# A fifth place for probabilities, half key blocks and interleaved query features in a four-layer attention kernel

## The chip, the cores and the metric

The kernel runs on one core of a Trainium2 chip. The metric is the device time of one execution in microseconds (us); several runs are taken and their median is used. The engines are named as in the profile: PE (TensorE) multiplies, PEld is its weight load, DVE (VectorE), ACT (ScalarE) and POOL (GpSimd) work element by element, SP (SyncE) issues most transfers.

## The reference

Four residual blocks follow one another on 2048 tokens of 512 features: A, B, A, B, with the same weights for both A and for both B. There are 32 heads of 16 features.

```python
def _A_ref(x, wqkv, wo):          # linear attention
    q, k, v = heads(x @ wqkv)
    phi = lambda t: jnp.where(t > 0, t + 1, jnp.exp(t)) + 1e-6
    pq, pk = phi(q), phi(k)
    kv = jnp.einsum("bhsd,bhse->bhde", pk, v)
    z = jnp.einsum("bhsd->bhd", pk)
    num = jnp.einsum("bhqd,bhde->bhqe", pq, kv)
    den = jnp.einsum("bhqd,bhd->bhq", pq, z)[..., None] + 1e-6
    return merge(num / den) @ wo

def _B_ref(x, wqkv, wo):          # causal attention in a window of 256
    q, k, v = heads(x @ wqkv)
    scores = jnp.einsum("bhqd,bhkd->bhqk", q, k) * (Dh ** -0.5)
    mask = (i - j >= 0) & (i - j < 256)
    p = _softmax(jnp.where(mask, scores, -1e9), axis=-1)
    return merge(jnp.einsum("bhqk,bhkd->bhqd", p, v)) @ wo

x = x + _A_ref(_layernorm(x), A_wqkv, A_wo)
x = x + _B_ref(_layernorm(x), B_wqkv, B_wo)
x = x + _A_ref(_layernorm(x), A_wqkv, A_wo)
x = x + _B_ref(_layernorm(x), B_wqkv, B_wo)
```

## The kernel before

The tokens are 16 tiles of 128. A Python class (`Plan`) lists every operation of the program with its engine or engines, what it reads and writes, and its PSUM banks (`Tile`); nothing loops on the chip. The order of all operations, the engine of each that has a choice, and the bank of each PSUM tile are not computed: they are read from a table of bytes packed in the source (`TABLE`, unpacked in `place`), so a new table is a new schedule. `synchronise` then puts the semaphore waits in. `WIDE` names DVE operations behind which POOL operations of a later place in the order wait.

The stages, with the lines of the profile:

- **First layer (A), keys** (`layer_a_keys`, 0 to about 47 us): for each tile a layer norm, transposed; key features (`tok`, L406) through phi (ACT L429, DVE L430 and L431), and sums over tokens (L481, L504). Query features (`feat`, L420) have the 128 features of one chunk on the partitions, chunk f being heads 8f to 8f+7.
- **Barrier** (`barrier`): the masked kv sum times the output weights gives a matrix M (one product for each chunk, L527; copied by L395). For each group G of four tiles the denominators are made in four column tiles of PE (L543), inverted (L547, L548) to 32 heads x 128 tokens per tile, and spread over the partitions by PE: 16 products on 32-row tiles fill four PSUM banks, one for each tile of tokens (L556). DVE multiplies the query features by that (L563, PSUM source).
- **Second layer (B), together with the next A keys** (`middle(2)`): for tile j the result of A is added (`a_out`, L406 and L574), normed and transposed by a DMA, and projected (L420). `b_scores` makes scores of 64 keys x 256 queries for two feature groups and two 64-key blocks on 32-row tiles (L638), exponentials over 1024 columns (ACT L648) into a place `P(j % rp)`, and the diagonal's mask (POOL L657 or DVE L658). `b_far` makes the last 64 queries of each key block's window (L712, exponentials L725, mask L743 or L744). `b_values` multiplies probabilities and values: for each of 16 head pairs one product for each of up to six key blocks of 64 keys x 2 heads (L764, 128 queries as weights, 34 columns: two heads of 16 values and a one). In the first block after the diagonal and in the farthest, half of the 128 queries meet zeros kept in columns 320 to 384 of each row. Then a reciprocal and a division (L775, L776), a transpose by DMA, the output product and the residual (L406, L574).
- **Second barrier**, then the **last layer (B)** (`middle(3)`): as above, but with `merged` set: the near scores skip 32 queries (224 instead of 256, exponentials of 896 columns), and `b_far` computes these with the far ones on 32-row, 64-column tiles (L715), twice as many products; DVE puts the near part in its place under the mask (L735). The probabilities have `rp = 4` places here, three in their own buffer and one (`P(3)`, tile name vp) over the finished keys and values of layer A.

SP's DMAs are one queue in program order: kB and vB copies of keys and values (L600, L619), transposes (L377), outputs (L931).

Of the kernel before, what the change touches and what calls it, by code (L numbers as in the profile page):

```python
# [11 lines left out]
P = 128  # L12
# [76 lines left out]
WIDE = ("E1", "xn", "mk", "mf")  # L89
# [128 lines left out]

def bass_view(x, free):

    return bass.AP(x.tensor, x.offset, [x.ap[0]] + free)


class Plan:
# [83 lines left out]
    def consts(self, after):  # L308
# [11 lines left out]
        pool("c4", lambda e: e.affine_select(out=K.bmask[:], in_=K.bmask[:], compare_op=ALU.is_ge, fill=0.0, base=0, pattern=[[-16, 8], [0, 16]], channel_multiplier=1), 152, 300, rd=[("bmask",)], wr=[("bmask",)])  # L320
        pool("c5", lambda e: e.affine_select(out=K.bmask[:], in_=K.bmask[:], compare_op=ALU.is_ge, fill=0.0, base=15, pattern=[[16, 8], [0, 16]], channel_multiplier=-1), 153, 300, rd=[("bmask",)], wr=[("bmask",)])

        pool("c6", zero(lambda: K.hot, 1.0), 154, 200, wr=[("hot",)])
        pool("c7", lambda e: e.affine_select(out=K.hot[:], in_=K.hot[:], compare_op=ALU.is_ge, fill=0.0, base=0, pattern=[[128, 4], [-16, 32]], channel_multiplier=1), 155, 300, rd=[("hot",)], wr=[("hot",)])
        pool("c8", lambda e: e.affine_select(out=K.hot[:], in_=K.hot[:], compare_op=ALU.is_ge, fill=0.0, base=15, pattern=[[-128, 4], [16, 32]], channel_multiplier=-1), 156, 300, rd=[("hot",)], wr=[("hot",)])
        pool("c9", zero(lambda: K.spread), 157, 1750, wr=[("spread",)])
        for tg in range(4):
            pool("c10", lambda e, tg=tg: e.affine_select(out=K.spread[:], in_=K.spread[:], compare_op=ALU.not_equal, fill=1.0, base=-32 * tg, pattern=[[-8, 4], [-1, 8], [0, 16]], channel_multiplier=1), 158, 760, rd=[("spread",)], wr=[("spread",)])
# [116 lines left out]
    def a_q(self, t, key):  # L445
        K = self
        ps = self.feat("q", t, lambda c, f: K.wA[:, c, f * P:(f + 1) * P], lambda c: K.XQ[:, c, t * P:(t + 1) * P], [("XQ", t), ("wAq",)], key)
        self.phi(ps, lambda: K.XQ[:, :, t * P:(t + 1) * P], [("XQ", t)], key + 0.1, 1)

    def a_kv(self, t, kv, z, key):  # L450
        K = self

        def put(e):
# [4 lines left out]
            for f in range(4):  # L458
                fs = slice(f * P, (f + 1) * P)
                m = e.matmul(K.ps(z)[:, f:f + 1], K.pk[:, t, fs], K.ones[:, 0:1], start=t == 0 and f == 0, stop=t == T - 1, skip_group_check=True)  # L460
# [4 lines left out]
    def layer_a_keys(self, ph, base):  # L465
# [33 lines left out]
        for q in range(4):  # L499
            def put(e, q=q):  # L500
                m = None
                for t in range(4 * q, 4 * q + 4):
                    for f in range(4):
                        m = e.matmul(K.ps(z)[:, f:f + 1], K.pk[:, t, f * P:(f + 1) * P], K.ones[:, 0:1], start=t == 0 and f == 0, stop=t == T - 1, skip_group_check=True)  # L504
# [5 lines left out]
    def barrier(self, ph):  # L510
# [12 lines left out]
        self.on("DVE", "kvm", lambda e: e.tensor_tensor(K.pqd[:, :, :], K.ps(kv).rearrange("p (f n) -> p f n", f=4), K.bmask[:].unsqueeze(1).to_broadcast([P, 4, P]), ALU.mult), key - 2, dve(512), rd=[("bmask",)], wr=[("pqd",)], ps=[kv])  # L523
        self.on("DVE", "zs", lambda e: e.tensor_tensor(K.zs[:], K.hot[:], K.ps(z)[:, 0:4].unsqueeze(2).to_broadcast([P, 4, 32]), ALU.mult), key - 2, dve(128), rd=[("hot",)], wr=[("zs",)], ps=[z])
        for f in range(4):
            ps = Tile(1, K.cls)
            self.pe("M", lambda e, f=f, ps=ps: e.matmul(K.ps(ps), K.pqd[:, f, :], K.wAo[:, f, :], start=True, stop=True), key - 2 + f * 0.01, 1, 512, rd=[("pqd",), ("wAo",)], ps=[ps])  # L527
            self.copy("Me", ps, lambda f=f: K.M[:, f, :], lambda ps=ps: K.ps(ps), key - 2 + f * 0.01, 512, wr=[("M", f)])
        for G in range(4):
# [19 lines left out]
            bc = [Tile(1, "S") for _ in range(4)]  # L549

            def put(e, G=G, bc=bc):
                m = None
                for f in range(4):
                    for tg in range(4):
                        rows = slice(32 * tg, 32 * tg + 32)
                        m = e.matmul(K.ps(bc[tg])[:, f * P:(f + 1) * P], K.spread[rows, f, :], K.rec[rows, G, :], start=True, stop=True, tile_position=(32 * tg, 0))  # L556
                return m

            self.pe("spread", put, k + 0.2, 1, 512, occ=245, mode=(32, 128), rd=[("rec", G), ("spread",)], ps=bc)
            for tg in range(4):  # L560
                t = 4 * G + tg
                x = lambda t=t: K.XQ[:, :, t * P:(t + 1) * P]
                self.on("DVE", "pqd", lambda e, x=x, b=bc[tg]: e.tensor_tensor(x(), K.ps(b).rearrange("p (f n) -> p f n", f=4), x(), ALU.mult), k + 0.3 + 0.01 * tg, dve(512), rd=[("XQ", t)], wr=[("XQ", t)], ps=[bc[tg]])  # L563
# [131 lines left out]
    def b_far(self, j, key):  # L695
# [33 lines left out]
        for fs in ((0, 1), (2, 3)) if merged else ():  # L729
            for b in range(2):  # L730
                def mk(e, b=b, fs=fs):
                    x = bass_view(K.P(sl)[:, fs[0], 0, 384 * b + 288:384 * b + 320], [[704, 8], [-256, 2], [1, 32]])
                    o = bass_view(K.P(sl)[:, fs[0], 0, 384 * b:384 * b + 64], [[704, 8], [32, 2], [1, 32]])
                    t = K.tri[:, 0, :].rearrange("p (a n) -> p a n", a=2).unsqueeze(1).to_broadcast([P, 8, 2, 32])
                    return e.tensor_tensor(o, x, t, ALU.mult)  # L735

                self.on("DVE", "mk", mk, key + 0.02 + 0.01 * b + 0.2 * fs[0], dve(512, "2x"), rd=[("P", sl, f, b, h) for f in fs for h in range(2)] + [("F", sl, 0), ("F", sl, 1), ("tri",)],
                        wr=[("P", sl, f, b, 2) for f in fs] + [("near", sl, b, fs[0])])
        for b in range(2):
# [7 lines left out]
            self.g.add("mf", engs, mk, key + 1.5 + 0.01 * b, rd=[("F", sl, 0), ("F", sl, 1), ("tri",)] + [("near", sl, b, 0), ("near", sl, b, 2)] * merged, wr=[("F", sl, b, 1)])  # L747

    def b_values(self, j, h, key):
# [23 lines left out]
        s = j % 2  # L773
# [380 lines left out]
```

## Time and profile before

| | |
|---|---|
| median of 3 runs | 406.92 us (406.59 to 408.15) |
| profiled execution, first to last instruction | 405.4 us |
| PE busy | 386.1 us, 95%, 7930 instructions |
| DVE busy | 333.6 us, 82%, 759 |
| ACT busy | 341.5 us, 84%, 439 |
| POOL busy | 149.2 us, 37%, 243 |
| granted PE clock | full throughout |

The profiled execution is one run of the program; its span leaves out about 1.5 us that the timed runs hold around it. Matmuls are pipelined and their ends modelled, so the start of the next instruction tells more of PE than the length of one. A mean share of busy time hides stages of different kind, so the profile is read by stretches. Numbers like L764 are lines of the kernel; in a group of instructions the columns are count, busy us, mean ns of one, and the idle time before them with what ended it.

### The profile page before, as it was taken

What the parts mean: (1) busy time and instruction counts of PE and PEld (TensorE: products, weight loads), DVE (VectorE), ACT (ScalarE), POOL (GpSimd) and SP (SyncE); (2) the same over time, 40 slices, a digit from 0 to 9 for tenths busy, and PEclk for the clock granted to TensorE, in tenths of its full rate; (3) what the DMA queues carried; (4) which work ended last, traced back from release to release, by engine and by line L of the source; (5) the groups of instructions that cost most, each with busy time, mean ns of one, the idle gap of its engine ahead of it and who ended that gap; (6) DMA issues with size and microseconds to landing.
All of it is one profiled execution on the core that took longest, in us unless ns stands there. A gap on an engine that the chain in (4) does not pass through costs nothing.

```text
span 405.4 us, 18074 instructions
## 1 busy us (share of the span) xinstructions
PE 386.1 (95%) x7930; PEld 263.9 (65%) x8004; DVE 333.6 (82%) x759; ACT 341.5 (84%) x439; POOL 149.2 (37%) x243
## 2 busy tenths in 40 slices
PE   8999999998999999999999999999999999999896
PEld 3644776766576566666666777677767775566665
DVE  6998898979998798887858789997898759776775
ACT  2655568998999999999998445999999999999994
POOL 3555624534363545541752213141132221232212
PEclk9999999999999999999999999999999999999999
DMA  8734216333253545353232000335224433344443
GB/s 250 243 66 128 82 41 127 106 80 92 71 94 69 122 97 101 63 129 81 62 79 56 20 2 12 96 83 135 69 57 108 110 76 75 82 118 94 115 124 107
DMA packets 67062, 37.75 MB, mean 93 GB/s; under 512 B 47688, under 2 KB 62152, under 8 KB 66984
## 3 DMA queue, kind: packets, MB, share of 16 engines
q1 hardware_dynamic: 66640, 35.67, 36.3%
q8 instruction: 63, 1.03, 1.2%
q0 software_dynamic: 336, 0.92, 0.7%
q14 instruction: 15, 0.12, 0.1%
q10 hardware_dynamic: 8, 0.00, 0.0%
HBM read 6.29 MB, written 2.10 MB: 21 GB/s over the span
## 4 chain that ended last, share of the span: by engine, by line
PE 76%; ACT 16%; DVE 5%; issue 2%; DMA 1%; ACTq 0%
PE ps L406 25%; PE ps L420 19%; PE ps L764 13%; ACT pb L648 10%; PE ps L638 6%; PE ps L481 3%; PE ps L715 2%; ACT pb L725 2%; ACT vp L648 2%; PE ps L712 1%; DMA xT<-xn 1%; PE ps L1067 1%; ACT vp L725 1%; PE ps L457 1%; DVE XQ L563 1%
## 5 line engine op out<-in xcount | busy, mean ns | idle before, releaser
L648 ACT ACTIVATE pb<-ps 128x1024 bf16<-128x1024 f32 (+3 forms) x224 | 198.4, 974 | 7.1 <-PE ps L638 5.5
L764 PEld LDWEIGHTS ps<-vB,pb 128*128 128x128 bf16 x2496 | 75.2, 96 | 10.4 <-issue 3.9
L764 PE MATMUL ps<-vB,pb 128*128 128x34 bf16 x2496 | 80.2, 177 | 0.3 <-DVE pb L744 0.2
L420 PE MATMUL ps<-xT,wBp 128*128 128x128 bf16 x1024 | 68.5, 219 | 0.9 <-DMA xT<-xn 0.6
L420 PEld LDWEIGHTS ps<-xT,wBp 128*128 128x128 bf16 x1024 | 58.8, 98 | 10.9 <-issue 4.5
L429 ACT ACTIVATE tE<-ps 128x512 bf16<-128x512 f32 x64 | 37.6, 605 | 26.3 <-PE ps L406 16.5
L743 POOL TENSOR_SCALAR_AFFINE_SELECT pb<-pb 128x1024 bf16<-128x1024 bf16 x32 | 36.9, 1152 | 53.8 <-DVE pb L735 37.6
L657 POOL TENSOR_SCALAR_AFFINE_SELECT pb<-pb 128x512 bf16<-128x512 bf16 x51 | 34.3, 673 | 48.4 <-ACT pb L648 20.6
L725 ACT ACTIVATE pb<-ps 128x1024 bf16<-128x1024 f32 x50 | 49.3, 1052 | 2.0 <-PE ps L715 1.0
L574 DVE TENSOR_TENSOR xres<-ps,xres 128x512 bf16<-128x512 f32 x63 | 42.9, 682 | 9.4 <-PE ps L406 9.1
L370 POOL TENSOR_TENSOR rs<-ve,negh 128x1 f32<-128x1 f32 x64 | 37.2, 581 | 32.1 <-DVE ve L369 27.5
L638 PE MATMUL ps<-XQ,kB 32*128 32x256 bf16 (+3 forms) x992 | 47.0, 264 | 1.7 <-ACT pb L648 0.5
L406 PE MATMUL ps<-wA,XQ 128*128 128x512 bf16 x179 | 45.7, 379 | 1.8 <-issue 0.8
L367 DVE BATCH_NORM_STATS2 stats<-xres 128x6 f32<-128x512 bf16 x64 | 43.8, 686 | 2.7 <-DMA xres<-in_A_x_dram 1.8
L420 PE MATMUL ps<-XQ,wA 128*128 128x128 bf16 x512 | 35.4, 219 | 0.1
L369 POOL TENSOR_SCALAR ve<-mv 128x1 f32<-128x1 f32 x45 | 11.5, 255 | 64.4 <-DVE mv L368 62.4
L420 PEld LDWEIGHTS ps<-XQ,wA 128*128 128x128 bf16 x512 | 30.6, 98 | 5.5 <-issue 0.7
L406 PE MATMUL ps<-wBv,xT 128*128 128x512 bf16 x108 | 30.1, 380 | 2.9 <-issue 1.4
L638 PEld LDWEIGHTS ps<-XQ,kB 32*128 32x128 bf16 x992 | 14.9, 92 | 26.4 <-ACT pb L648 8.4
L406 PE MATMUL ps<-wBo,oT 128*128 128x512 bf16 x103 | 28.6, 380 | 3.1 <-issue 1.9
L406 PE MATMUL ps<-M,XQ 128*128 128x512 bf16 x114 | 29.7, 380 | 1.3 <-issue 0.6
L406 PEld LDWEIGHTS ps<-wA,XQ 128*128 128x128 bf16 x192 | 17.0, 97 | 19.6 <-issue 2.1
(128 smaller groups left out, 569.1 us busy)
## 6 DMA issues: line engine op xcount, KB each, us to landing
vB<-vS SPq DMA_DIRECT2D x64, 136.0 KB, 2.6
kB<-vp SPq DMA_DIRECT2D x64, 128.0 KB, 2.2
wA<-in_A_wqkv_dram SPq DMA_DIRECT2D x3, 512.0 KB, 5.0
out_dram<-xres SPq DMA_DIRECT2D x9, 128.0 KB, 2.8
xres<-in_A_x_dram SPq DMA_DIRECT2D x2, 512.0 KB, 4.9
pb<-in_B_wqkv_dram SPq DMA_DIRECT2D x1, 1024.0 KB, 5.6
out_dram<-xres POOLq DMA_DIRECT2D x7, 128.0 KB, 2.2
xres<-in_A_x_dram SPq DMA_DIRECT2D x3, 256.0 KB, 4.7
```

The source lines that it names most:

```text
L367: self.on("DVE", "stats", lambda e: e.bn_stats(K.stats[:, t, :], K.xres[:, t, :]), key, dve(512), rd=[("xres", t)], wr=[("stats", t)])
L370: self.pow = self.on("POOL", "pow", lambda e: e.tensor_tensor(K.rs[:, t, :], K.ve[:, t, :], K.negh[:], ALU.pow), key + 0.03, (640, 690), r ...
L406: m = e.matmul(K.ps(ps), lhs(c), rhs(c), start=c == 0, stop=c == 3)
L420: m = e.matmul(K.ps(ps)[:, f * P:(f + 1) * P], w(c, f), xT(c), start=c == 0, stop=c == 3)
L429: self.on("ACT", "E", lambda e: e.activation(K.tE[:, s, :], K.ps(ps), ACT.Exp, bias=0.0), key, act(512), wr=[("tE", s)], ps=[ps])
L574: self.on("DVE", "res", lambda e: e.tensor_tensor(K.xres[:, t, :], K.ps(po), K.xres[:, t, :], ALU.add), key, dve(512), rd=[("xres", t)], w ...
L638: m = e.matmul(K.ps(ps[gq])[:, ns * i:ns * i + ns], K.kB[rows, j % 4, 2 * f + b, :, :], K.XQ[rows, f, q:q + ns], start=True, stop=True, ti ...
L648: return e.activation(out(h, ns).rearrange("p (f g) c -> p f g c", f=n), i, ACT.Exp, bias=0.0, scale=0.25)
L657: return e.affine_select(out=x, in_=x, compare_op=ALU.is_ge, fill=0.0, base=1, pattern=[[0, 4 * n], [2, 64]], channel_multiplier=-1)
L725: return e.activation(o.rearrange("p (f g) b c -> p f g b c", g=2), i, ACT.Exp, bias=0.0, scale=0.25)
L743: return e.affine_select(out=x, in_=x, compare_op=ALU.is_ge, fill=0.0, base=-2, pattern=[[0, 16], [-2, 64]], channel_multiplier=1)
L764: m = e.matmul(K.ps(ps)[:, 34 * u:34 * u + 34], K.P((b // 2) % rp)[:, f, gq % 2 * 2 + gq // 2, o:o + P], K.vB[:, (b // 2) % 4, b % 2, r, : ...
```

## The change

1. **Interleaved query features.** A chunk c now holds every fourth feature, so each chunk has four features of all 32 heads. The weights of q and the keys for z are read with a step of four elements; the masks in `consts` follow. The reciprocals are then the same for all four chunks.
2. **Spreading.** For group G = 0 PE spreads with four full products into one bank. For G = 1, 2, 3 of both barriers SP copies the 32 rows of reciprocals to 128 partitions of a free SBUF buffer (four copies per group), and DVE multiplies from there (`pqs`, all operands in SBUF). `pqs` is in `WIDE`.
3. **M** is made by 16 products on 32-column tiles instead of four full ones.
4. **Half key blocks** (`b_pairs`): for tiles j from 2 on (not the last tile of the last layer) four full key blocks go to two PSUM banks; the two blocks with half their queries live are multiplied as 64-column tiles, side by side.
5. **Last layer**: `merged` only for j from 3 on; five places for probabilities, the fifth over layer A's weights, later keys and the spread matrix, so it is cleared after these are last read; DVE or POOL may do the near mask.
6. **A new table** of orders, engines and banks.

```diff
-WIDE = ("E1", "xn", "mk", "mf")
+WIDE = ("E1", "xn", "mk", "mf", "pqs")
+COPIED = ((1, 2, 3), (1, 2, 3))
+SHARED = ((), range(3, 14))
...
+def every(x, c):
+    return x.rearrange("p (n c) -> p c n", c=4)[:, c, :]
...
-        ps = self.feat("q", t, lambda c, f: K.wA[:, c, f * P:(f + 1) * P], ...
+        ps = self.feat("q", t, lambda c, f: every(K.wA[:, c, 0:512], f), ...
...
-                m = e.matmul(K.ps(z)[:, f:f + 1], K.pk[:, t, fs], K.ones[:, 0:1], ...
+                m = e.matmul(K.ps(z)[:, f:f + 1], every(K.pk[:, t, :], f), K.ones[:, 0:1], ...
...
-            self.pe("M", lambda e, f=f, ps=ps: e.matmul(K.ps(ps), K.pqd[:, f, :], K.wAo[:, f, :], start=True, stop=True), ...
+                for f in range(4):
+                    m = e.matmul(K.ps(ps)[32 * f:32 * f + 32, :], K.pqd[:, c, 32 * f:32 * f + 32], K.wAo[:, f, :], start=True, stop=True, tile_position=(0, 32 * f))
...
+            if G in COPIED[ph - 1]:
+                for tg in range(4):
+                    room = lambda tg=tg: K.pqd[:, tg, :]
+                    def put(e, G=G, tg=tg, room=room):
...
+                        i = bass.AP(src.tensor, src.offset + 32 * tg * ss + P * G, [[ss, 32], [0, 4], [1, P]])
+                        return e.dma_start(o, i)
+                    self.on("SP", "bd", put, ...)
+                    self.on("DVE", "pqs", lambda e, t=t, room=room: e.tensor_tensor(x(t), x(t), wide(room()), ALU.mult), ...)
+                continue
...
-                for f in range(4):
-                    for tg in range(4):
-                        rows = slice(32 * tg, 32 * tg + 32)
-                        m = e.matmul(K.ps(bc[tg])[:, f * P:(f + 1) * P], K.spread[rows, f, :], K.rec[rows, G, :], start=True, stop=True, tile_position=(32 * tg, 0))
+                for tg in range(4):
+                    m = e.matmul(K.ps(bc)[:, tg * P:(tg + 1) * P], K.spread[:, tg, :], K.rec[:, G, :], start=True, stop=True)
...
+    def b_pairs(self, j, key):
+        banks = [Tile(1, K.cls) for _ in range(2)]
+        full = ((2 * j, 0), (2 * j - 1, 64), (2 * j - 2, 128), (2 * j - 3, 192))
...
+                            for b, c in some:
+                                o = 384 * (b % 2) + c
+                                m = e.matmul(K.ps(banks[f // 2])[:, 34 * u:34 * u + 34], prob(b, f, gq)[:, o:o + P], val(b, f, gq), ...
...
+                        for half, b in ((0, 2 * j - 4), (1, 2 * j + 1)):
+                            o = 384 if half else 256
+                            m = e.matmul(K.ps(banks[h])[64 * half:64 * half + 64, 34 * u:34 * u + 34], prob(b, f, gq)[:, o:o + 64], val(b, f, gq), start=False, stop=True, tile_position=(0, 64 * half), ...
...
-        self.merged = last
+        self.last = last
-        self.rp = 4 if last else 3
+        self.rp = 5 if last else 3
...
         for j in range(T):
+            self.merged = j in SHARED[last]
...
+            if j >= 2 and not end:
+                self.b_pairs(j, base + j + 0.5 + par["k_pv"])
```

More of the change, by code (lines that the diff above doesn't have):

```diff
@@ L919, in middle @@
                 self.b_far(j, base + j + 0.8)
-            for h in range(2):
-                (self.b_values_end if last and j == T - 1 else self.b_values)(j, h, base + j + (h + 1) / 2 + par["k_pv"])
+            end = last and j == T - 1
+            if j >= 2 and not end:
+                self.b_pairs(j, base + j + 0.5 + par["k_pv"])
+            else:
+                for h in range(2):
+                    (self.b_values_end if end else self.b_values)(j, h, base + j + (h + 1) / 2 + par["k_pv"])
             if not last:
```

245 lines of the change are left out of this document (150 added, 95 removed).

## The prediction

> **What bounds it now.** I read the stages first (busy time of each engine in eight stretches), since the change touches some stages and not others.
>
> ```profile
> core 0: us, PE busy (x) PEld busy (x) DVE busy (x) ACT busy (x) POOL busy (x), PEclk, DMA share, GB/s
> 0.00:47.00 47.00, 45.49 (x391) 25.30 (x397) 39.25 (x100) 21.55 (x37) 25.13 (x59) 1.00 0.57 166
> 47.00:62.00 15.00, 14.68 (x204) 10.66 (x207) 14.78 (x31) 10.77 (x19) 4.38 (x10) 1.00 0.12 36
> 62.00:222.00 160.00, 153.23 (x3177) 103.00 (x3209) 134.54 (x299) 154.33 (x183) 73.39 (x111) 1.00 0.40 89
> 222.00:244.00 22.00, 21.78 (x377) 16.02 (x380) 17.08 (x37) 9.94 (x19) 5.26 (x9) 1.00 0.07 14
> 244.00:262.00 18.00, 17.53 (x299) 12.32 (x299) 17.42 (x39) 12.64 (x21) 4.43 (x9) 1.00 0.17 48
> 262.00:322.00 60.00, 58.54 (x1488) 43.33 (x1493) 51.60 (x121) 56.30 (x73) 17.46 (x22) 1.00 0.38 94
> 322.00:385.00 63.00, 58.19 (x1578) 40.78 (x1586) 45.43 (x103) 61.44 (x75) 15.10 (x18) 1.00 0.41 94
> 385.00:405.40 20.40, 16.62 (x441) 12.51 (x443) 13.51 (x33) 14.56 (x20) 4.02 (x7) 1.00 0.42 118
> ```
>
> The reader is to see two bounds. The keys and barriers (up to 62, and 222 to 262) are PE's: 97 to 99% busy, ACT far below. The two window-attention stretches have both at the rim: from 62 to 222 PE stands still 6.8 us and ACT 5.7; from 262 to 322 PE 1.5 and ACT 3.7; from 322 to 385 PE 4.8 and ACT only 1.6. DVE has 25.5 us free from 62 to 222. The clock is full, so no gate is in it. The chain of waits, the whole of it and one stretch, says the same:
>
> ```profile
> PE 76%; ACT 16%; DVE 5%; issue 2%; DMA 1%; ACTq 0%
> ...
> 349.51 1.94 ACT pb L725 x2
> 351.45 6.48 ACT pb L648 x8
> ```
>
> Exponentials run back to back there, 6.48/8 = 0.81 us each; no PE saving shortens that stretch. So I count PE savings first, then what ACT lets through.
>
> **Half key blocks.** The 27 query tiles (j 2 to 15 of the second layer, 2 to 14 of the last) have six key blocks; two of them hold 64 live queries each. Before, each of 16 head pairs takes six full products, 96 per tile; after, 64 full ones and 16 pairs of half products, side by side in two column halves.
>
> ```profile
> 91.06 1.21 PE ps L764 x48
> ...
> 342.34 1.30 PE ps L764 x48
> ...
> 290.13 0.33 PE L715 MATMUL ps<-XQ,kB 32*64 32x64 bf16 x32
> ...
> 290.13 0.71 PE L715 MATMUL ps<-XQ,kB 32*64 32x64 bf16 x64
> 290.76 1.37 PE L764 MATMUL ps<-vB,pb 128*128 128x34 bf16 x48
> 292.10 0.37 PE L638 MATMUL ps<-XQ,kB 32*128 32x224 bf16 x8
> ```
>
> The first two rows are of the chain, the others of PE's timeline; the row with x32 is the stretch 290.13 to 290.266 asked for alone. 48 products follow at 1.21/48 = 25 ns; entered from another tile shape they take 0.1 us more (1.30), so a change of shape costs about 0.1 us. The two full blocks that go are 32 × 25 ns = 0.80 us per tile. No row shows a half product. The nearest is the far score on 64-column tiles (eight at a time): 32 start in 0.136 us, four rounds, 34 ns per tile and round, weight load included, with 64 moving columns where the half block has 34. Over all 64 it is (0.63 - 0.1)/8 = 66 ns a round. So a pair costs 25 ns (PE's spacing in L764) to 66 ns; I take 30, between the spacing and the burst, since it moves fewer columns: 16 × 30 = 0.48 us. Added changes of shape: one per tile if both half groups stand together beside a score group, four if each stands alone between full ones; I take two, 0.2 us. Net 0.80 - 0.48 - 0.20 = 0.12 us per tile, 3.2 us over 27; bounds +0.3 (25 ns, one change) and -0.66 (66 ns, four changes).
>
> [...]
>
> **Interleaved q features.** Every chunk now holds four features of all 32 heads, so one 128x128 reciprocal serves all four chunks.
>
> ```profile
> L563 DVE TENSOR_TENSOR XQ<-ps,XQ 128x512 bf16<-128x512 f32 x32 | 20.0, 683 | 1.6 <-PE ps L556 1.5
> L735 DVE TENSOR_TENSOR pb<-pb,tri 128x512 bf16<-128x512 bf16 x44 | 17.4, 413 | 2.1 <-ACT pb L648 1.4 <-ACT pb L725 0.3
> L556 PE MATMUL ps<-rec,spread 32*128 32x128 bf16 x128 | 3.2, 216 | 0.3 <-ACT vp L725 0.2
> L420 PE MATMUL ps<-XQ,wA 128*128 128x128 bf16 x512 | 35.4, 219 | 0.1
> L543 PE MATMUL ps<-XQ,zs 128*32 128x128 bf16 x128 | 3.2, 219 | 0.0
> kB<-vp SPq DMA_DIRECT2D x64, 128.0 KB, 2.2
> vB<-vS SPq DMA_DIRECT2D x64, 136.0 KB, 2.6
> ...
> 57.94 0.36 PE ps L556 x16
> 58.30 0.02 issue
> 58.33 2.48 DVE XQ L563 x4
> 60.81 0.32 DVE xn L371
> 61.13 0.03 DVE stats L367
> 61.16 4.27 DMA xT<-xn
> ...
> 107.56 0.89 PE ps L420 x16
> ```
>
> Six of eight spreads (0.36 us each by the chain, and a change of shape) become 24 small copies: 6 × 0.45 = 2.7 us off PE. The two that stay become four full products, 4 × 56 ns (0.89/16, last row), 0.2 us less each: 0.4. DVE's 24 scalings have all operands in SBUF and 16 bits; nearest is L735 at 413 ns against 683: 24 × 0.27 = 6.5 us off DVE. M takes 16 products of 512 columns in four column tiles for four; L543, 160 products in the same tiles with its eps rows, is 3.2 us for 128, half a full product's 56 ns each, so four side by side cost about one. I take 0.2 us lost per barrier (two changes of shape; bounds 0 and, if they ran one by one at four times 56 ns, 12 × 0.22 = 2.6).
>
> The copies go into SP's queue: each issue stands before the kB, vB and transposed tiles queued behind it, and waits for its reciprocal. Landing 2.2 to 2.6 us replaces 0.36 us of spread. In the second barrier's later groups and from 62 on, work for several tiles lies ahead; at 58 us the chain runs through it (rows from 57.94): there the path could grow by 2.2 + 0.6 (an issue, by my estimate a quarter of the landing) - 0.4 - 4 × 0.27 = 1.3 us, unless the order starts that group earlier. I take 0.5 lost; bounds 0 and 6 × 1.3. Banks: a spread held four and now one or none, which only helps. The q weights and the keys' sums are read with a step of four elements; I cost this at nothing, because the 56 ns stream covers a load that L764 shows done in 25. POOL must wait for the new DVE form: 24 waits of 0.4 us, POOL idle half the time, nothing. Smaller constants on POOL: nothing, before 47 us it is half idle.
>
> **First three tiles apart, fifth place.**
>
> ```profile
> L648 ACT ACTIVATE pb<-ps 128x1024 bf16<-128x1024 f32 x120 | 114.8, 1039 | 3.9 <-PE ps L638 2.4
> L648 ACT ACTIVATE pb<-ps 128x896 bf16<-128x896 f32 x88 | 74.6, 943 | 1.8 <-PE ps L638 1.8
> 108.45 0.34 PE ps L712 x32
> 348.81 0.68 PE ps L715 x64
> ...
> 294.19 0.62 PE L420 MATMUL ps<-XQ,wA 128*128 128x128 bf16 x8
> 299.13 3.43 ACT L648 ACTIVATE pb<-ps 128x896 bf16<-128x896 f32 x4
> L884 POOL MEMSET vp<- 128x1024 bf16 x1 | 1.0, 951 | 0.7 <-DVE tE L430 0.7
> ```
>
> Apart, ACT does 24 exponentials 0.1 us longer, 2.3 us more; PE's far scores 0.34 for 0.68, three times 0.34 = 1.0 less, given back by a third in longer near scores (estimate); twelve L735 masks become L657 or L658 ones, which POOL may take. ACT's extra lies in 244 to 280, where it has 5.4 us idle up to 262: nothing on the path. The fifth place lets exponentials run one tile further ahead; it is worth nothing to the 3.7 us that ACT idles from 262 to 322, and I take 0.7, near the lower end, since ACT's waits there are for scores, not places. Its room lies over the q weights, so all q features must be done before tile 4: they end at 294.8, tile 4's first exponential is at 299.1 (both of the timeline), and the clearing of a place's pad takes 1 us, which fits.
>
> **New orders.** They can't be read from the table. Bounds by the stages above: the 5.7 us that ACT idles from 62 to 222 closed at best, as much again opened at worst; I take none by itself.
>
> **Sum.** PE's savings: 62 to 222, 14 × 0.12 + two spreads 0.9 = 2.6; last layer 13 × 0.12 + 1.35 + 0.7 = 3.6; first barrier 0.65 - 0.2 - 0.5 = 0; second 0.2 - 0.2 = 0. ACT lets 2.0 of the 2.6 through (its idle 5.7 us bounds it, and DVE, relieved by 3.2 us per barrier, can take over evictions), and 2.3 of the 3.6, as 322 to 385 is ACT's; with 0.7 for the place the sum is 5.0 us. The profile's span of 405.4 becomes 400.4; the median of the runs is 406.92, 1.5 above the span, so 401.9.
>
> **Rivals.**
> 1. ACT holds: it is 96 to 98% busy in both stretches, has no instruction taken off and 2.3 us added. Then PE only waits longer and the time is 405 to 408. For: the stretch from 349 on. Against: PE leads the chain for 76%.
> 2. Slower, by the half products: at 66 ns a pair and four changes of shape PE gains 0.66 × 27 = 17.8 us, less the other 3 or 4: 421. Above 51 ns with two changes it decides: 27 × (16 × 0.051 - 0.6) = 5.8 us, which eats the 3.8 us of other savings and passes 0.5%. Against: the burst of 34 ns.
>    [...]
> 3. The stepped weight loads: over 56 ns a load, 512 q products lengthen; at 100 ns by 22 us, 429. No row has a stepped load; that full loads fit in 25 ns speaks against.
> 4. Broadcasts late at each of six groups: 6 × 1.3 = 8 us, 410.
> 5. Orders that use DVE's relief fully, and pairs at 25 ns with one change: 27 × 0.3 = 8 us plus 3.8, cut by ACT's idle to about 10: 397.
>
> **Numbers.** 0.5% is 2.0 us, about what a measurement can tell from no change. Forecast 0.56 (its own range 398.5 to 404.5), ACT holds 0.21, half products dear 0.09, stepped loads 0.04, late broadcasts 0.03, the large gain 0.07. Faster 0.63, same 0.21, slower 0.16. The range 397.5 to 409 leaves out the stepped loads, most of the dear half products and of the large gain.
>
> **What would show it.** Half pairs: 16 half products in 0.24 us plus 0.1, with no new wait of DVE for PE. Scaling at 0.41 us for 24. PE's sum from 62 on 6 us lower with ACT's share higher. A chain that is mostly ACT, or PE waiting for the broadcast, or q products apart by more than 56 ns, makes me wrong.

## The result and the profile after

Predicted 401.9 us; measured 410.59 us, median of 12 runs (408.01 to 413.23). The kernel before, beside it on the same chip, took 407.04 us in 12 runs (406.43 to 409.45). The ratio is 1.0075, with a 95% interval of 1.0054 to 1.0097: slower by 3 us, outside the range of 397.5 to 409. The profiled execution has a span of 408.1 us; that of before had 405.4. Three runs further on were slow (432.8 us of `a_outs`, 421.5 of `a_load`, 413.5 of `a_noout`): the medians count them, the ratios don't.

The stages of the changed kernel, in the same stretches as before (busy time of PE, weight load, DVE, ACT, POOL; granted clock; DMA share):

```profile
core 0: us, PE busy (x) PEld busy (x) DVE busy (x) ACT busy (x) POOL busy (x), PEclk, DMA share, GB/s
62.00:222.00 160.00, 158.06 (x3201) 101.80 (x3201) 135.45 (x316) 156.24 (x186) 67.61 (x100) 1.00 0.41 93
262.00:322.00 60.00, 59.04 (x1412) 42.44 (x1411) 48.68 (x110) 56.94 (x69) 23.04 (x40) 1.00 0.46 97
322.00:385.00 63.00, 59.54 (x1551) 40.24 (x1551) 42.40 (x92) 59.84 (x72) 26.10 (x46) 0.97 0.40 90
385.00:408.10 23.10, 17.68 (x465) 12.69 (x461) 13.97 (x36) 14.73 (x20) 6.11 (x12) 0.99 0.49 116
```

PE's busy time can't be compared with the rows of before: that trace has 504 products of 512 columns (L406), this one all 572 (L413), and each missing record leaves a hole. From 62 to 222 most of the 6.8 us that PE seems to stand still in before lies beside such holes; with all records it is 1.9 us here. So PE had less room before than the prediction read.

Up to 322 nothing is won and little is lost. I followed the 64 divisions (DVE, one for each half of a query tile, o<-ps) through both traces: the first four come 0.5 to 2.0 us late (in the first layer PE waits 2.1 us for a transpose), and from the ninth on they lie within 2 us on either side of those of before, until 384 us. The last one is 2.2 us late. So in the profile the loss is made at the end. From 322 on the granted clock is 0.97 and 0.99 where all of before was 1.00. Only the 0.97 falls on work: the 0.99 comes from a stretch at half from 407.4 on, and PE's last product starts at 404.2.

Two terms of the sum came as forecast (DVE's scaling; the q features that are read with a step; both as minimum/median/maximum length in ns, with the wait for copies):

```profile
L579 DVE TENSOR_TENSOR XQ<-XQ,pqd x24: 361/416/424, 61.6 to 338.2; 128x512 bf16<-128x512 bf16 x24
  DMA pqd<-rec: 0.3, 1
...
L427 PE MATMUL ps<-XQ,big x512: 219/219/250, 9.2 to 293.9; 128*128 128x128 bf16 x171
```

And this is the end of the chain (start, us, what; L804 are the full products of probabilities and values, L823 the half products):

```profile
384.72 0.30 PE ps L667 x8
385.03 0.36 PE ps L823 x16
385.38 0.90 PE ps L804 x32
386.29 0.33 PE ps L667 x8
386.61 0.29 PE ps L823 x11
386.90 0.85 issue
387.76 0.24 PE ps L823 x5
...
394.64 0.79 PE ps L804 x32
395.43 0.36 PE ps L823 x16
...
396.98 0.28 PE ps L804 x11
397.25 0.97 issue
398.22 0.69 PE ps L804 x21
```

Two readings. A half group of 16 takes 0.36 us, and a full group behind a tile of another shape 0.90 in place of 0.79 (behind a half group as behind the scores of L667): that is the change of shape. And twice PE stops in the middle of a group ("issue": it waits for nothing that the profile shows). A third such stop lies at 341.4. PE's waits from 322 on:

```profile
PE ps L823 <- issue: 1.6, 2, 0.9
PE ps L744 <- DVE o L836: 1.5, 2, 1.0
PE ps L804 <- issue: 1.0, 1, 1.0
```

Measured between the starts of neighbouring instructions the three stops are 0.88, 1.04 and 1.15 us long, 3.1 in all. The trace points at what they may be. A queue that the page calls "q8 instruction" moves 62 packets, 1.02 MB, so 16 KB each; PE and its weight load have 15841 records, an estimated 256 for each packet (15841/62; 16151/63 in before). All three stops stand at record numbers of these two that leave 192, to within two, when divided by 256 (12736, 15040, 15552), and each ends 1.4 to 1.6 us after such a packet has ended. So I read them as PE waiting for its next instructions and call them stops for instructions; no row names the cause. The trace of before has none of them in this layer. Behind the first, at 342.6, the clock is at half for 3.4 us.

### The profile page after: what moved, and what is told of

It is laid out like the page before. It is cut to its first block, busy times and chain, and to the rows that moved or that the text cites. A ratio compares the mean times of both kernels' runs of the same rounds, so it can differ in the third digit from the quotient of the medians.

```text
span 408.1 us, 17833 instructions
## 1 busy us (share of the span) xinstructions
PE 392.6 (96%) x7812; PEld 261.0 (64%) x7812; DVE 326.1 (80%) x752; ACT 343.7 (84%) x433; POOL 159.8 (39%) x282
## 3 DMA queue, kind: packets, MB, share of 16 engines
q8 instruction: 62, 1.02, 1.1%
## 4 chain that ended last, share of the span: by engine, by line
PE 67%; ACT 18%; DMA 6%; DVE 6%; issue 2%; POOL 0%; SPq 0%; POOLq 0%
PE ps L413 23%; PE ps L427 17%; ACT pb L677 11%; PE ps L804 8%; PE ps L667 7%; ACT pb L754 3%; PE ps L823 3%; PE ps L488 3%; ACT big L677 2%; DMA xT<-xn 2%; PE ps L744 1%; DVE stats L374 1%; PE ps L741 1%; DMA XQ<-big 1%; PE ps L856 1%
## 5 line engine op out<-in xcount | busy, mean ns | idle before, releaser
L677 ACT ACTIVATE pb<-ps 128x1024 bf16<-128x1024 f32 (+3 forms) x200 | 181.3, 1004 | 4.0 <-PE ps L667 3.1
L804 PE MATMUL ps<-vB,pb 128*128 128x34 bf16 x1408 | 52.3, 178 | 1.5 <-issue 1.0
L804 PEld LDWEIGHTS ps<-vB,pb 128*128 128x128 bf16 x1408 | 47.6, 96 | 8.2 <-issue 2.5
L413 PE MATMUL ps<-big,XQ 128*128 128x512 bf16 x192 | 49.6, 380 | 2.1 <-DMA XQ<-big 2.1
L667 PE MATMUL ps<-XQ,kB 32*128 32x256 bf16 (+3 forms) x992 | 47.6, 266 | 1.5 <-ACT pb L677 0.5
L677 ACT ACTIVATE big<-ps 128x896 bf16<-128x896 f32 (+2 forms) x48 | 41.3, 942 | 3.7 <-PE ps L667 3.6
L427 PE MATMUL ps<-XQ,big 128*128 128x128 bf16 x512 | 35.3, 220 | 0.0
L835 DVE RECIPROCAL rc<-ps 128x16 f32<-128x16 f32 x64 | 16.2, 253 | 23.9 <-PE ps L823 21.0
L427 PEld LDWEIGHTS ps<-XQ,big 128*128 128x128 bf16 x512 | 31.4, 114 | 5.7 <-issue 1.2
L776 POOL TENSOR_SCALAR_AFFINE_SELECT pb<-pb 128x1024 bf16<-128x1024 bf16 x24 | 27.9, 1161 | 16.7 <-ACT pb L754 6.8
L413 PE MATMUL ps<-wBv,xT 128*128 128x512 bf16 x128 | 34.3, 381 | 0.0
L413 PE MATMUL ps<-M,XQ 128*128 128x512 bf16 x128 | 34.0, 381 | 0.0
L413 PE MATMUL ps<-wBo,oT 128*128 128x512 bf16 x124 | 32.8, 380 | 0.5 <-DMA oT<-o 0.3
```

Source lines behind the costliest of these rows:

```text
L413: m = e.matmul(K.ps(ps), lhs(c), rhs(c), start=c == 0, stop=c == 3)
L427: m = e.matmul(K.ps(ps)[:, f * P:(f + 1) * P], w(c, f), xT(c), start=c == 0, stop=c == 3)
L667: m = e.matmul(K.ps(ps[gq])[:, ns * i:ns * i + ns], K.kB[rows, j % 4, 2 * f + b, :, :], K.XQ[rows, f, q:q + ns], start=True, stop=True, ti ...
L677: return e.activation(out(h, ns).rearrange("p (f g) c -> p f g c", f=n), i, ACT.Exp, bias=0.0, scale=0.25)
L776: return e.affine_select(out=x, in_=x, compare_op=ALU.is_ge, fill=0.0, base=-2, pattern=[[0, 16], [-2, 64]], channel_multiplier=1)
L804: m = e.matmul(K.ps(banks[f // 2])[:, 34 * u:34 * u + 34], prob(b, f, gq)[:, o:o + P], val(b, f, gq), start=own != 1 and f % 2 == 0 and gq ...
```

## Experiments

Beside each kernel the kernel before ran on the same chip; its medians were 406.8 to 407.7 us, and each ratio is to it.

### Which engine sets the pace

`b_skip`, `b_actless` and `b_both` (kernel before) and `a_actless` (changed kernel) leave work out: `b_skip` the two half-live key blocks, `b_actless` and `a_actless` 32 columns of many exponentials.

```diff
 b_skip:    + if j >= 2:
            +     blocks = [(b, c) for b, c in blocks if c not in (-64, 256)]
 b_actless, a_actless (exponentials of the near scores, rp <= j < 14):
            - x -> [[ns, n], x, [1, ns]]
            + x -> [[ns, n], x, [1, ns - 32]]
 b_both:    both of b_skip and b_actless
 b_flip:    27 evictions of ACT (bqe, bke, bve, ve, recb) are given to DVE
```

> The kernel before, with the two half-live key blocks left out for every tile from 2 on (four of six products for each head pair; their contribution is missing from the output): 27 tiles x 32 products x 25 ns = 21.6 us less on PE, with no new tile shapes. This is more than any form of half blocks can save. Theory A (ACT's exponentials set the pace from about 100 to 385 us): the time falls only where PE is alone, in the last tiles (2 x 0.8 us) and by part of ACT's idle time there (some 6 us): 402 to 405 us. Rival P (PE sets the pace): it falls by 15 us or more, to 386 to 392 us.

> The kernel before, with the near exponentials of the middle tiles 32 columns shorter (1024 to 896 in the second layer, tiles 3 to 13, 896 to 768 in the last, tiles 4 to 13; the columns left out keep old values): 168 x 0.107 = 18 us off ACT, nothing else touched. Theory A (ACT sets the pace from 100 to 385): faster by what PE's own idle lets through, 5 to 10 us, 397 to 402 us. Rival O (the pace is the fixed order and the waits between engines, not ACT's load): under 3 us, 404 us or more.

> The changed kernel with the same exponentials shortened (tiles 3 to 13, and 5 to 13 in the last layer: 160 x 0.107 = 17 us off ACT). Theory A: with ACT relieved PE binds, and the 3.8 us net that the change takes off PE come out: this kernel gains 2 to 4 us more than the kernel before does by the same edit, and stands within 1.5 us of it. Rival O: it gains as little as the other, and the distance of 3.5 us stays.

> The kernel before with both earlier reductions at once: the two half-live key blocks are left out of every product with the values (21.6 us less PE), and 18 us of ACT's exponentials over far keys are left out. Alone they gave 1.2 to 1.9 us and 1.0 to 1.3 us. Theory C (two engines share the bound: what one gives up the other's work takes the room of): only the pair moves the time, by 10 us or more, 397 us or less. Theory L (neither engine's load sets the pace between the stages; the written order and its chains of score, exponential, mask, product and division do): the two gains only add, 403.5 to 405.5 us.

> The kernel before, with the 27 copies out of PSUM that ACT does after the first score group given to DVE, in the same order; nothing else. ACT does 27 x about 0.6 us less (16 us, perhaps half of it inside the stretches where it never rests), DVE 27 x 0.69 us more. Theory A: 4 to 10 us faster, 397 to 403 us. Rival P, or DVE's order as the limit: no change or slower, 406 to 411 us.

| kernel | median us | ratio (95%) |
|---|---|---|
| b_skip | 405.58 | 0.9954 (0.9930 to 0.9979) |
| b_actless | 406.68 | 0.9967 (0.9944 to 0.9989) |
| b_both | 398.58 | 0.9767 (0.9737 to 0.9798) |
| a_actless | 408.47 | 1.0018 (0.9988 to 1.0048) |
| b_flip | 421.62 | 1.0378 (1.0349 to 1.0408) |

One row of the stages (322 to 385), in the order `b_skip`, `b_actless`, `b_both`; before it was PE 58.19, ACT 61.44:

```profile
322.00:385.00 63.00, 55.91 (x1392) 36.74 (x1390) 45.60 (x105) 60.79 (x75) 15.10 (x18) 0.97 0.38 90
```
```profile
322.00:385.00 63.00, 58.19 (x1591) 41.28 (x1600) 45.70 (x104) 56.75 (x74) 15.10 (x18) 1.00 0.43 93
```
```profile
322.00:385.00 63.00, 56.66 (x1496) 37.81 (x1503) 49.39 (x113) 60.81 (x80) 17.23 (x21) 1.00 0.49 103
```

Taken from one engine alone, the work turns into idle time of that engine, and the other stays nearly as it was: PE's 58.2 when ACT has less to do, ACT's 60.8 when PE has less. With both relieved ACT gets through 80 operations in this stretch where it got through 75, and the last division comes 10.6 us earlier, against 0.9 and 0.5. The waits from 62 to 385 show where the idle time goes: PE waits for exponentials before it makes the next scores (before, then `b_skip`), and ACT waits for scores (before, then `b_actless`):

```profile
PE ps L638 <- ACT pb L648: 0.5, 2, 0.3
```
```profile
PE ps L638 <- ACT pb L648: 5.0, 15, 0.5
```
```profile
ACT pb L648 <- PE ps L638: 5.5, 12, 0.7
```
```profile
ACT pb L650 <- PE ps L638: 13.6, 32, 1.4
```

So the two bounds don't share out a saving, each holds most of it: -1.9, -1.3 and together -9.5 us by the ratios. The written threshold was 397 us; the median of 398.58 missed it by 1.6, but 403.5 and more, where the gains would just add, is far off.

The 1.9 us of `b_skip` hides more. In its profile the divisions are 3.3 us ahead of before until a stretch at half clock, and only 1.5 ahead once it is over:

```profile
371.60:375.00 3.40, 3.40 (x39) 2.85 (x36) 1.48 (x3) 2.20 (x3) 0.42 (x1) 0.50 0.64 143
```

Over the runs at full clock alone (table below; 0.999 or more) `b_skip` gains 4.0 us (three runs), `b_actless` 0.7 (eleven) and `b_both` 9.5 (four). In the profile of `b_actless` a stop for instructions, shown further down, takes 0.9 us of its lead of 1.3. Even so the two alone stay well below the pair.

`a_actless` is 2.3 us faster than the changed kernel by the ratios, 1.0 more than the same edit gives before; 2 to 4 more were written for the case that ACT alone holds. `b_skip` (402 to 405 written) and `b_flip` missed what was written for them. In `b_flip` DVE was no free helper. The divisions fall 6 us behind across the second barrier, where DVE had little room, and PE now waits for it there (222 to 266):

```profile
PE ps L420 <- DVE vp L395: 1.7, 1, 1.7
PE ps L383 <- DVE xn L371: 1.3, 2, 1.0
```

### The parts by themselves

```diff
 a_full:    half products made whole (128 query columns, o = 320 or 256, no tile_position)
 a_merged:  - SHARED = ((), range(3, 14))
            + SHARED = ((), range(0, 14))
 b_apart (in before):
            + self.merged = last and j >= 3
 b_int:     before + interleaved q with its copies, order of before, copies put 8 places behind the reciprocal
 a_order:   all parts of the change, order, engines and banks of before
 b_int2:    before + interleaved q without copies (COPIED = ((), ())), order of before
 a_nocopy:  changed kernel, COPIED = ((), (3,)), own order
```

> The changed kernel with the half products made whole again (the same 16 instructions per group, 128 columns instead of 64, zeros in the half that isn't live; same order, same engines). By the trace a half group is 0.24 us and two changes of shape 0.2 us, a whole one 16 x 25 ns = 0.40 us: PE's work stays within 0.04 us per group, 54 groups, 2 us. Theory A: within 1 us of the changed kernel (410.6 us). Theory F (PE runs out of instructions in the dense half groups): its stops of 0.9 to 1.1 us inside a group get rarer, 408 to 410 us. Rival H (half products were a gain that something else hides): slower, 412 to 414 us.

> The changed kernel with the first three query tiles of the last layer merged again (three operations moved by a few places, one mask to DVE; else the same order): 24 exponentials 0.1 us shorter, 2.3 us off ACT; PE's far scores 1.0 us more. Theory M: 1.5 to 2.3 us faster, 408.3 to 409.1 us. Theory B: within 0.7 us of the changed kernel, 410 to 411 us, since ACT has 5.4 us idle where these tiles are.

> The kernel before with only the far queries of the first three tiles of the last layer taken apart (12 more masks of their own, no other edit, the order kept). In the changed kernel the opposite edit lost 2.9 us. If taking apart is a gain by itself: 404 to 405.5 us. If that loss came from the changed kernel's order, which was written for tiles apart: 406 to 409 us.

> The kernel before with the interleaved q features alone: the strided weight reads, four spread products in place of sixteen, the copies of the reciprocals in 24 of 32 places, the interleaved M. No half products, no fifth place, no tile taken apart, and the order of the kernel before, with each copy 8 places behind its reciprocal and the multiplications as far behind as in the changed kernel. Theory O (the parts are worth about what the prediction gave them and the new orders lose it again): 404 to 406 us. Theory P (the parts themselves are worth nothing, the time goes in waits on the copies and the denser tail): 406.5 to 409 us.

> All the parts of the change (interleaved q, half products, fifth place, first three tiles apart), but the order, engines and PSUM banks of the kernel before for every operation that both have; new operations stand beside their neighbours. Theory O (the new orders lose what the parts gain): 403 to 406 us, below the changed kernel by 4 us or more. Theory P (the parts bring nothing, order or not): 408 to 412 us, no less than the changed kernel.

> The kernel before with the interleaved q features, but without any copies: strided weight reads, four spread products of 128 columns in place of sixteen, DVE's multiplication from PSUM as before, the interleaved M; the order, engines and banks of the kernel before. This is the interleave alone without new waits on the queue. By the prediction's prices PE does 3.1 us less at the two barriers. Theory I (this is a gain): 404 to 406 us. Theory J (PE's barrier work lies beside other work, or the denser reads cost elsewhere): 406.5 to 408.5 us.

> The changed kernel in its own order, but 20 of the 24 copies of reciprocals are made by TensorE again (four products of 128 columns in one bank for each group of four tiles) and DVE multiplies from PSUM; the last group of the second barrier keeps its copies, since the fifth place lies on the spread matrix. DVE does 20 x 0.27 = 5.4 us more, SP issues 20 copies less. Theory K (the copies' issue and landing cost what DVE gains): 407 to 410 us. Theory D (DVE's 5.4 us were a gain): 412 to 415 us.

| kernel | median us | ratio (95%) |
|---|---|---|
| a_full | 410.32 | 1.0093 (1.0072 to 1.0114) |
| a_merged | 413.50 | 1.0130 (1.0098 to 1.0161) |
| b_apart | 409.74 | 1.0049 (1.0028 to 1.0070) |
| b_int | 435.04 | 1.0677 (1.0646 to 1.0709) |
| a_order | 436.55 | 1.0710 (1.0674 to 1.0745) |
| b_int2 | 421.62 | 1.0365 (1.0346 to 1.0384) |
| a_nocopy | 424.13 | 1.0415 (1.0383 to 1.0447) |

By the medians the half products are worth nothing. In the chain of `a_full` the same groups, now whole, read (first; below it the changed kernel at the place of 390.93):

```profile
388.98 0.31 PE ps L667 x8
389.28 0.50 PE ps L823 x16
389.78 0.87 PE ps L413 x4
390.65 0.28 PE ps L667 x8
390.93 0.90 PE ps L804 x32
391.83 0.40 PE ps L823 x16
```
```profile
389.25 0.90 PE ps L804 x32
390.15 0.36 PE ps L823 x16
```

A whole group takes 0.40, or 0.50 behind a tile of another shape; a half group takes 0.36 behind either, and a full group behind it pays the change. Both kernels have the same products in the same order, so their starts can be compared: of the 52 places with half products 46 have no wait in either trace, and there PE is 1.6 us faster in all with half products, 0.03 to 0.06 us at most places. For all 52 that is an estimated 1.8 us. At full clock the changed kernel is 1.4 us faster than `a_full` (408.9 on three runs, 410.2 on five of six). So the runs leave two readings: PE's 1.8 us don't reach the end, or they do and the half clock, 9 of 12 runs against 1 of 6, takes them back.

Taking three tiles apart is a gain of 2 to 3 us in the order that was written for it (`a_merged`, where three operations also moved by a few places, against the changed kernel; its 413.50 missed both ranges written for it) and a loss of 2 in the order that wasn't (`b_apart`). The four hybrids missed every expectation. They don't price the interleave, they price an order that doesn't fit. In `b_int`, PE's waits from 62 to 165:

```profile
PE ps L427 <- DMA xT<-xn: 4.8, 1, 4.8
PE ps L413 <- DVE XQ L579: 3.1, 1, 3.1
...
PE ps L667 <- DMA kB<-big: 1.2, 1, 1.2
```

Before, the longest of these was 0.6 us. The copies go before keys and transposes in SP's queue (four of them, 0.6 us each, held the first keys back by some 2 us), and the scaling waits for them on DVE. In `b_int2` there are no copies, but one bank now holds the reciprocals of four tiles. DVE's order is that of before, and the four scalings stand in one block there too; they now start 0.72 us apart instead of 0.60, the block at 101.5 lasts 2.8 us, and for the mask behind it PE waited 2.6 us by the profile. Why PE didn't wait at this place before isn't shown. `a_nocopy` has its scalings moved up into blocks, so its 13.5 us above the changed kernel don't tell the copies' worth either, beyond the 5.4 us of theory D. What the interleaved q is worth by itself stays open.

### Stops for instructions

```diff
 a_shift:   start-up matmuls: 9 of 512 columns -> 5 of 512 and 68 of 34 (128 more PE instructions)
 a_outs:    13 output transfers moved up, to 25 places behind their residual
 a_noout, b_noout (outputs of j 0 to 14):
            - K.out[0, j * P:(j + 1) * P, :],    K.xres[:, j, :]
            + K.out[0, j * P:(j + 1) * P, 0:64], K.xres[:, j, 0:64]
 a_load, b_load (the same outputs, ahead of each):
            + e.dma_start(scratch rows of 1024 columns, K.xres[:, j, :] twice)
```

> The changed kernel with 128 more PE instructions at the start (four of nine warm-up products of 512 columns replaced by 68 of 34 columns, while PE waits for the input): every later PE instruction comes 128 places later in the stream; no work is changed. Theory F (the three stops of 0.9, 1.0 and 1.1 us inside groups without a wait, all at a place of the stream that is 192 modulo 256, are PE waiting for its next 256 instructions): the stops move to other instructions, again 256 apart, and the time changes by up to 2.5 us either way, 408 to 411.5 us. Rival W (those stops are waits for data that the trace doesn't show): the same three places stop as long as before, and the time stays at 410.6 us.

> The changed kernel with the 13 output transfers that stood far behind their data in the order moved to shortly behind it (25 places after the residual sum); engines and all else as they were. Theory B (the new order issues seven output transfers between 390.3 and 396.2 us, where the 16 DMA engines are then 0.8 to 0.9 busy, and these hold back the transposed o tile, landing in 5.1 us there instead of 2.5, the v copies in 4.9 instead of 2.6, and PE's instructions): the last tiles get 1.5 to 2.5 us back, 408 to 409.2 us. Rival M (the three unmerged tiles put 2.3 us on ACT, and that is what comes out at the end): no change, 410.3 to 410.8 us.

> The changed kernel, but each of the first fifteen output transfers of the last layer moves 64 of 512 columns (an eighth of the bytes; the rest of those rows is not written). Same instructions on every engine. Theory F (in the last layer TensorE runs out of instructions because the 16 KB packets that bring them queue behind the output transfers; three such stops of 0.9 to 1.1 us and the half clock behind one of them make up the loss): the stops are gone or under 1 us in all, and the time falls by 3 to 5 us to 405.5 to 407.5. Theory G (the stops come from the density of the matmul stream, not from other transfers): stops of 2 us or more stay, 409 to 411.5 us.

> The control: the kernel before with the same cut of its first fifteen output transfers to an eighth of their bytes. Its profile had no stops, so both theories F and G: 406 to 407.5 us, within 1 us of the kernel before.

> The kernel before with three times the output bytes in the last layer: ahead of each of the first fifteen output transfers the same rows are sent twice to a scratch tensor in memory by one more transfer from the same queue. TensorE's stream is the same instruction for instruction; GpSimd issues some 13 transfers more, which can delay a mask by about 1 us each. Theory F (TensorE's instruction packets queue behind transfers): stops for instructions appear in the last layer, 1 us or more in all, 408.5 to 411 us, and the clock falls below full more often than in 9 of 86 runs. Theory G (only the density of the matmul stream makes the stops): no stops, 407 to 408.5 us.

> The changed kernel with the same three times the output bytes. With an eighth of them it ran at 408.7, with all at 410.6 us. Theory F: more and longer stops, 4 us or more in all, 412 to 416 us. Theory G: stops of 2 to 3.5 us as before, 410 to 411.5 us.

| output bytes in the last layer | before | changed |
|---|---|---|
| an eighth | 407.05, 1.0005 (0.9987 to 1.0023) | 408.73, 1.0033 (1.0009 to 1.0056) |
| all | 407.04 | 410.59, 1.0075 (1.0054 to 1.0097) |
| three times | 412.17, 1.0114 (1.0079 to 1.0150) | 417.74, 1.0242 (1.0180 to 1.0304) |
| all, moved up (a_outs) | | 411.28, 1.0073 (1.0049 to 1.0097) |
| all, stream shifted (a_shift) | | 414.60, 1.0200 (1.0157 to 1.0242) |

`a_shift` had three stops again, at stream numbers 12736, 15040 and 15808: multiples of 256 apart from those of the changed kernel, two at the very same numbers, though other instructions stand there now. That fits the reading of a load in blocks of 256, and not a property of the instructions. The profiled run is the fastest of six that spread from 411.0 to 416.9; why the median is 4 us above the changed kernel I can't say. `a_outs` thinned the DMA share between 395 and 400 (0.47, was 0.88) and kept two stops of 1.16 and 0.97 us: the burst of outputs at the end isn't alone to blame.

Cutting or adding output bytes moves the stops, though not by itself. PE's waits for "issue" in the middle of product groups, first in `a_noout` (one row left of the two that stood there), then in `b_load`, each from 322 on:

```profile
PE ps L823 <- issue: 0.8, 1, 0.8
```
```profile
PE ps L764 <- issue: 1.5, 2, 1.2
...
PE ps L638 <- issue: 0.6, 1, 0.6
```

With an eighth of the outputs' bytes the changed kernel keeps one stop (at 341.7, 1.0 us) and is 1.7 us faster by the ratios, between what was written for theory F and for theory G. With three times the bytes the kernel before, whose PE stream is the same, gets stops of 0.47, 0.90 and 1.40 us. In its chain:

```profile
379.70 0.29 PE ps L638 x5
379.99 0.65 issue
380.64 0.29 PE ps L638 x3
...
385.18 0.47 PE ps L764 x19
385.65 1.23 issue
386.88 0.28 PE ps L764 x5
```

Its divisions, 0.7 us ahead of before up to 355, are 0.2 behind after the first stop and 2.5 behind after the last. So with more transfers such stops come up in this kernel, as theory F has it, and the divisions move. But more bytes aren't needed. `b_actless`, with the PE stream and the output bytes of before, stops at the very place of the last one above:

```profile
382.53 0.47 PE ps L766 x19
383.00 0.97 issue
383.96 0.28 PE ps L766 x5
```

`b_flip` and `b_apart`, also with the bytes of before, have two stops each in the last layer (0.7 to 1.1 us). By that reading, which block comes late hangs on timing as well, and one profile for each kernel can't part the two.

The 5 us of `b_load` are no price of stops either. In the profile the last residual is 3.4 us later than before (406.07 against 402.70), PE having waited 1.5 us for a transpose and 0.7 for values as well; the other 3.9 us of the longer span lie behind it, where the last transfers land (at 410.9; in before at 404.5). In `a_load`, whose runs fall into three at 415.0 and three at 420.5 to 421.5, the biggest item in the profile (415.0) is another again, a copy of values that comes 3.2 us late:

```profile
PE ps L897 <- DMA vB<-vS: 3.2, 1, 3.2
```

### What the clock adds

The granted clock sorts the runs into those with a full clock (0.999 or more) and those with one or more stretches at half. Over all runs that count in the ratios:

| kernel | runs at full clock, mean us | below, mean us |
|---|---|---|
| before | 86 of 96, 407.4 | 10, 409.8 |
| changed | 3 of 12, 408.9 | 9, 410.9 |
| a_noout | 3 of 11, 406.8 | 8, 409.3 |
| b_noout | 11 of 12, 407.1 | 1, 409.7 |
| b_skip | 3 of 12, 403.4 | 9, 405.9 |
| b_load | 0 of 5 | 5, 412.6 |

Runs below full clock are 2.1 to 2.6 us longer. That is not all the clock's: one stretch of 3.4 us at a granted 0.50 holds back an estimated 1.7 us of work (3.4 × 0.50), and cost 1.8 in `b_skip` above. The sorting is rough, too: the granted clock is that of the whole span, and in the profiled runs of `b_load` and `a_shift` (0.998) the only half stretch lies behind PE's last product.

In several profiles the half clock begins where a stop for instructions ends: in the changed kernel at 342.6 after the stop up to 342.3, in `a_full` at 345.1 after 345.1, in `a_outs` at 395.0 after 395.0. Not behind every stop: `b_load` had three, of up to 1.4 us, `b_actless` one of 1.15 and `b_apart` two, of 0.7 and 0.8, and PE worked at a full clock throughout. And `b_skip`, where PE has 864 products less and no long stop, is below full clock in 9 of 12 runs. What sets the clock is not shown.

## Why the prediction was wrong

**Right: the prices.** Sixteen half products take 0.36 us (0.24 and 0.1 forecast), one pair every 32 ns (30 forecast), so rival 2 is out. DVE's scaling is 416 ns (413 forecast) in 24 places; the q features with stepped weight loads start 56 ns apart in both traces (median), so rival 3 is out; DVE waits 0.3 us in all for a copy, so rival 4 is out in this order. That rival 4 named 410 us, nearly the measured time, is luck. ACT has 2.2 us more (2.3 forecast), with six instructions fewer. The sign "PE's sum from 62 on 6 us lower" can't be read, as the trace of before misses records.

**Too large: half key blocks, "added changes of shape".** A change costs what I took, but I set the saving against full products that enter without one. In `a_full` a whole group also pays 0.10 behind another shape. Against whole products in the same order the net is an estimated 1.8 us of PE's work, not 3.2, and the medians don't show it (410.32 against 410.59).

**Wrong: the sum, "ACT lets 2.0 of the 2.6 through".** This is the step that failed. I let a saving on PE pass wherever ACT had some idle time. It passed 4.3 of 6.2 us, over two thirds. `b_skip` removed 864 products, 21.6 us at 25 ns, and got 1.9 us, or 4.0 at full clock: a tenth to a fifth. At that rate the 6.2 us of PE savings are worth 0.5 to 1.1. What I read as two engines at the rim with some room each is two engines that need each other's work at each tile: PE's relief mostly makes it wait for exponentials (5.0 us in `b_skip`, 0.5 before), and ACT's for scores (13.6 in `b_actless`, 5.5 before). The chain's 76% PE was no evidence against rival 1; the share says who was last, not who would be last next.

**Missing: what it costs to be denser.** Nothing in the sum stood for the three stops (3.1 us in the changed kernel's profile), or for the clock. At full clock the changed kernel is 1.5 us behind before (408.9 against 407.4, three runs only), and with an eighth of the output bytes 0.3 ahead (406.8, again three runs, against 407.1). That fits the stops, two of three being gone there, but doesn't show them to be the cause. Being below full clock in 9 of 12 runs rather than 10 of 96 adds 2.1 × 0.75 - 2.4 × 0.10 = 1.3 us. 1.5 and 1.3 are the 2.8 us between the means (410.4 and 407.6); this splits the difference and doesn't prove what made either part. If both are put aside, nothing measurable is left of the change, which is rival 1's answer (405 to 408), though ACT alone is not what holds.

**Not tested alone:** the fifth place, and the new orders; `a_order` shows only that the old order can't carry the new parts. So where the 3 us come from is argued, not shown; that the savings hardly pass is shown. **Open:** why the changed kernel has three stops with its own outputs and the kernel before none in its profile. Half products aren't it: `a_full` has three stops as well, of 0.68, 1.07 and 0.73 us.

No version here beats both kernels with the whole computation; the kernel before remains the fastest.

## What to carry to other kernels

Where two engines hand each tile to and fro, a saving on one of them can be worth little until the other is relieved too: leave work out of each alone and of both, and take the three numbers before you count instructions. A part that needs waits of its own is only as good as the order around it; put into an old order it can cost far more than it saves (28 us in `b_int`). And look at the instruction queue and at the clock of each run before you explain a few microseconds at the end of a kernel.

## What the runs showed of the hardware

- PE stopped inside product groups without a wait that the profile shows: 0.88, 1.04 and 1.15 us in the changed kernel, at record numbers that are multiples of 256 apart to within two, each stop ending 1.4 to 1.6 us after a 16 KB packet of the queue "q8 instruction". With three times the output bytes there were three in the last layer of a kernel that had none (`b_load`: 0.47, 0.90 and 1.40 us); with its own bytes `b_actless` had one (1.15 us). That PE waits for instructions there is a reading.
- The stretch at half clock (0.50 granted) lasted 3.4 us in the changed kernel, from 342.6, and in `b_skip`, from 371.6, where it set the divisions back by 1.8 us. It began where a stop ended in the changed kernel, `a_full` and `a_outs`; in `b_load` and `b_actless` none followed stops of up to 1.40 and 1.15 us. With 864 products less on PE it was more frequent (9 of 12 runs below full clock in `b_skip`, 10 of 96 before).
- Two half products side by side on column halves start every 32 ns (changed kernel, median of the starts; (0.36 - 0.1)/8 = 32 by the chain), one whole one every 25.
